# Decoding attention on one core: heads software-pipelined across the engines, K loaded one head ahead

## The chip, the core, the metric

One core of a Trainium2 chip. The metric is device time in microseconds (us) of one execution; lower is better. The kernel before takes 2669.79 us (median of 4 runs, 2669.45 to 2670.34). Repeats agree within 0.1%, so a few us can be seen, but only just.

## The reference

Two independent attention blocks (A and B) for one decoding step; their outputs are concatenated.

```python
# B=8 batches, 1 query, D=1024, H=32 heads, Sk=4096 keys, Dh=128, bfloat16
q = (x @ wq).reshape(B, 1, H, Dh).transpose(0, 2, 1, 3)
scores = einsum("bhqd,bhkd->bhqk", q, k_cache) * Dh ** -0.5
p = softmax(scores)
o = einsum("bhqk,bhkd->bhqd", p, v_cache)
out = o.transpose(0, 2, 1, 3).reshape(B, 1, H * Dh) @ wo
```

Every element of K and V is used once. Per head, K is 8 tiles of 1 MB (one a batch), and so is V. Over 64 heads that is 1.07 GB, read from memory once.

## The kernel before

One loop over heads n = 0..63. All loads are issued by SyncE (SP) on one queue. K tiles go into a ring of NK = 6 slots, V tiles into a ring of NV = 8. DVE transposes each K tile, PE multiplies it with q, then the softmax of the head goes DVE - PE - DVE - PE - ACT - DVE, then PE multiplies with V (pv), ACT evicts and scales, and PE projects with wo.

```python
# SP: all loads, in order
load_group(first[0])                       # wq of the first 4 heads: 8 DMAs of 128 KB
wait(sp, s_const, 1)                       # x_sb is zeroed by GpSimd first
... x ...
for n in range(NH):
    for b in range(Bsz):                   # K of head n
        t = n * Bsz + b
        wait(sp, s_tr, t - NK + 1)         # slot free: the tile NK back is transposed
        sp.dma_start(knat[:, t % NK, :], kc[b, h]...)
    ...                                    # every 4th head: wq; each head: wo, 256 KB
    for b in range(Bsz):                   # V of head n
        wait(sp, s_pv, t - NV + 1)         # slot free: the tile NV back has been multiplied
        sp.dma_start(vnat[:, t % NV, :], vc[b, h]...)

# PE, head n:    qk(n); max and bias matmuls; row sums; prep(n+1); pv(n); o^T; projection
# DVE, head n:   8 x transpose K; max; max of rows; transpose of e; reciprocal
```

Below, K(n,b) and V(n,b) are the tiles of head n and batch b, qk(n) and pv(n) are the two products of a head, pv(n,b) is the part of one batch.

## Time and profile before

| what | value | where it is read |
|---|---|---|
| time | 2669.79 us | runs |
| bytes read | 1107 MB, 415 GB/s over the span | page |
| DMA engines' busy share from 20 to 2650 us | 1.00 to 1.02 | windows |
| PE busy | 75% | page |
| DVE idle, waiting for a K tile | 1065 us | waits |
| full rate begins | about 10.6 us | windows of 1 us |

The page of the kernel before: busy time of the engines; then GB/s in 40 equal slices of the span; bytes; the chain of waits; and the two costliest groups (busy us, mean ns | idle us before them, and what ended the idle time).

```profile
PE 2009.5 (75%) x10880; PEld 729.3 (27%) x10880; DVE 1292.0 (48%) x781; ACT 263.3 (10%) x727; POOL 7.7 (0%) x17
...
GB/s 371 417 420 421 417 421 417 420 421 416 421 416 421 420 417 420 416 421 421 415 420 417 420 420 415 421 416 420 418 419 420 414 421 413 421 420 418 420 421 348
...
HBM read 1107.33 MB, written 0.03 MB: 415 GB/s over the span
...
DMA 81%; DVE 10%; SPq 6%; PE 2%; issue 1%; POOL 0%; ACT 0%; DVEq 0%; POOLq 0%
...
L249 DVE STREAM_TRANSPOSE kt<-knat 128x2048 f32<-128x2048 f32 x512 | 1170.9, 2303 | 1119.1 <-DMA knat<-in_B_k_cache_dram 536.7
L334 PE MATMUL ps<-kt,lpad 128*128 128x512 bf16 x4096 | 1021.6, 394 | 229.4 <-DVE kt L249 227.7
```

No compute engine is near full, and the chain of waits is DMA for 81%. DVE, which touches each K tile first, idled 1119 us, mostly for K tiles to land. The slices are at 413 to 421 GB/s except the first (371) and the last (348).

The windows view of the kernel before splits that up. Columns: stretch, its length, busy us (and count) of PE, PEld, DVE, ACT and POOL, granted PE clock, DMA busy share, GB/s.

```profile
0.00:10.00 10.00, 0.00 (x0) 0.00 (x0) 4.71 (x13) 0.00 (x0) 7.69 (x17) 1.00 0.35 108
10.00:40.00 30.00, 20.13 (x165) 7.52 (x165) 19.77 (x11) 4.78 (x12) 0.00 (x0) 1.00 1.00 413
40.00:60.00 20.00, 15.69 (x103) 5.66 (x99) 4.50 (x4) 2.66 (x7) 0.00 (x0) 0.86 1.01 421
60.00:70.00 10.00, 8.69 (x36) 3.17 (x34) 8.81 (x5) 0.00 (x0) 0.00 (x0) 0.93 1.01 422
70.00:100.00 30.00, 21.69 (x133) 7.89 (x132) 10.52 (x9) 3.90 (x11) 0.00 (x0) 0.92 1.01 420
100.00:2640.00 2540.00, 1925.60 (x10355) 698.62 (x10354) 1239.97 (x739) 248.05 (x688) 0.00 (x0) 0.93 1.01 419
```

Of these, only the first 10 us run far below the rest: 108 GB/s. The timeline of the start says why. Columns: start us, us, engine, line, operation, count, and in brackets the idle time before it and what ended it; SPq lines are DMA issues.

```profile
0.81 3.70 SPq L171 DMA_DIRECT2D wq_sb<-in_A_wq_dram  x8
...
8.16 0.20 POOL L225 TENSOR_SCALAR_AFFINE_SELECT selrow<-ones_bf 128x16 bf16<-128x16 bf16 x1
...
8.39 0.34 SPq L179 DMA_DIRECT2D x_sb<-in_A_x_dram  x1
...
9.10 9.85 SPq L189 DMA_DIRECT2D knat<-in_A_k_cache_dram  x8
...
18.82 3.65 PE L334 MATMUL ps<-kt,lpad 128*128 128x512 bf16 x16 [1.51 <-ACT lpad L424]
...
19.47 8.79 SPq L202 DMA_DIRECT2D vnat<-in_A_v_cache_dram  x8
```

The queue issues wq, then waits until GpSimd finishes its constants at 8.36 us (L225), issues x, and only at 9.10 us K. The first qk matmul runs at 18.82 us. V(0) is issued straight behind K(0), all eight tiles within 9 us.

The waits of the queue's own sequencer in the kernel before (us in total, times, longest):

```profile
SPq L189 <- DVE kt L249: 1189.8, 271, 15.9
```

The queue waits only for slots of K; it never once waits for a slot of V.

The Trainium skill ("DMA: Bandwidth & Descriptors", section Specifications) names a fabric ceiling of 435 GB/s and an HBM limit of about 358 GB/s per core, which it works out as half of what two cores share. This trace runs at 419 to 422 GB/s for 2.6 ms with only this core at work, so the second figure did not bind here; the measurement decides. That the limit is the 16 DMA engines and not the one queue in front of them is read from their busy share alone (1.00 to 1.02).

### The profile page before, as it was taken

What the parts mean: (1) busy time and instruction counts of PE and PEld (TensorE: products, weight loads), DVE (VectorE), ACT (ScalarE), POOL (GpSimd) and SP (SyncE); (2) the same over time, 40 slices, a digit from 0 to 9 for tenths busy, and PEclk for the clock granted to TensorE, in tenths of its full rate; (3) what the DMA queues carried; (4) which work ended last, traced back from release to release, by engine and by line L of the source; (5) the groups of instructions that cost most, each with busy time, mean ns of one, the idle gap of its engine ahead of it and who ended that gap; (6) DMA issues with size and microseconds to landing.
All of it is one profiled execution on the core that took longest, in us unless ns stands there. A gap on an engine that the chain in (4) does not pass through costs nothing.

```text
span 2667.7 us, 26152 instructions
## 1 busy us (share of the span) xinstructions
PE 2009.5 (75%) x10880; PEld 729.3 (27%) x10880; DVE 1292.0 (48%) x781; ACT 263.3 (10%) x727; POOL 7.7 (0%) x17
## 2 busy tenths in 40 slices
PE   6777777777777777777777777777777777777777
PEld 2222222222222222222222222222222222222222
DVE  5454544545535445354453544535535355363553
ACT  1001100011000110110101101011010100101001
POOL 1000000000000000000000000000000000000000
PEclk9998999999999989999999999999999899999989
DMA  9999999999999999999999999999999999999998
GB/s 371 417 420 421 417 421 417 420 421 416 421 416 421 420 417 420 416 421 421 415 420 417 420 420 415 421 416 420 418 419 420 414 421 413 421 420 418 420 421 348
DMA packets 175316, 1109.09 MB, mean 416 GB/s; under 512 B 19504, under 2 KB 35920, under 8 KB 44128
## 3 DMA queue, kind: packets, MB, share of 16 engines
q1 hardware_dynamic: 175136, 1107.41, 100.5%
q8 instruction: 86, 1.41, 0.2%
q14 instruction: 30, 0.25, 0.0%
q10 hardware_dynamic: 64, 0.03, 0.0%
HBM read 1107.33 MB, written 0.03 MB: 415 GB/s over the span
## 4 chain that ended last, share of the span: by engine, by line
DMA 81%; DVE 10%; SPq 6%; PE 2%; issue 1%; POOL 0%; ACT 0%; DVEq 0%; POOLq 0%
DMA knat<-in_B_k_cache_dram 39%; DMA knat<-in_A_k_cache_dram 37%; DVE kt L249 10%; SPq L189 3%; DMA vnat<-in_A_v_cache_dram 3%; DMA vnat<-in_B_v_cache_dram 2%; SPq L202 1%; SPq L171 1%; PE ps L334 1%; PE ps L289 0%; PE ps L372 0%; SPq L197 0%; POOL lpad L211 0%; ACT o_sb L452 0%; PE ps L394 0%
## 5 line engine op out<-in xcount | busy, mean ns | idle before, releaser
L249 DVE STREAM_TRANSPOSE kt<-knat 128x2048 f32<-128x2048 f32 x512 | 1170.9, 2303 | 1119.1 <-DMA knat<-in_B_k_cache_dram 536.7
L334 PE MATMUL ps<-kt,lpad 128*128 128x512 bf16 x4096 | 1021.6, 394 | 229.4 <-DVE kt L249 227.7
L372 PE MATMUL ps<-vnat,pq_sb 128*4 128x512 bf16 x4096 | 848.9, 433 | 119.8 <-DMA vnat<-in_A_v_cache_dram 61.3
L334 PEld LDWEIGHTS ps<-kt,lpad 128*128 128x128 bf16 x4096 | 367.3, 99 | 875.5 <-DVE kt L249 449.4
L372 PEld LDWEIGHTS ps<-vnat,pq_sb 128*4 128x4 bf16 x4096 | 292.2, 94 | 646.5 <-issue 152.1
L452 ACT ACTIVATE o_sb<-ps,rlo_sb 128x512 bf16<-128x512 f32 x128 | 80.9, 683 | 880.8 <-PE ps L372 880.8
L437 ACT ACTIVATE bias_sb<-ps 128x1 f32<-128x1 f32 x64 | 11.0, 171 | 1362.2 <-PE ps L347 1362.2
L253 DVE TENSOR_REDUCE m_sb<-ps 128x1 bf16<-128x512 f32 x64 | 44.4, 694 | 128.7 <-PE ps L334 128.7
L383 PE MATMUL ps<-selrow,o_sb 128*128 128x4 bf16 x512 | 22.6, 166 | 86.9 <-ACT o_sb L452 86.9
L261 DVE STREAM_TRANSPOSE pq_sb<-e_sb 128x512 bf16<-128x512 bf16 x64 | 45.5, 711 | 83.7 <-ACT e_sb L441 83.7
L424 ACT ACTIVATE lpad<-ps 32x32 bf16<-32x32 f32 x256 | 77.9, 304 | 70.3 <-PE ps L306 65.6
L354 PE MATMUL ps<-l1m_sb,maskcg 128*32 128x2 f32 x512 | 16.5, 188 | 90.5 <-ACT l1m_sb L445 90.5
L342 PE MATMUL ps<-ident,m_sb 128*1 128x128 bf16 x64 | 13.9, 217 | 50.3 <-DVE m_sb L253 50.3
L383 PEld LDWEIGHTS ps<-selrow,o_sb 128*128 128x128 bf16 x512 | 17.0, 96 | 119.0 <-ACT o_sb L452 119.0
L441 ACT ACTIVATE e_sb<-ps,bias_sb 128x512 bf16<-128x512 f32 x64 | 44.0, 687 | 2.1
L289 PE MATMUL ps<-wq_sb,xT_sb 128*8 128x512 bf16 x128 | 39.6, 466 | 0.0
L394 PE MATMUL ps<-wo_sb,oT_sb 128*8 128x512 bf16 x128 | 24.9, 386 | 17.1 <-ACT oT_sb L456 17.1
L354 PEld LDWEIGHTS ps<-l1m_sb,maskcg 128*32 128x32 f32 x512 | 11.0, 118 | 95.9 <-ACT l1m_sb L445 95.9
L306 PE MATMUL ps<-ident,q_pad 128*32 128x8 bf16 x1024 | 17.4, 170 | 24.9 <-DVE rlo_sb L264 24.2
L347 PE MATMUL ps<-scalecol,negm 128*32 128x1 bf16 x256 | 12.0, 177 | 23.9 <-DVE negm L257 23.9
L257 DVE TENSOR_REDUCE negm<-ps 1x16 bf16<-1x128 f32 x64 | 18.0, 281 | 19.8 <-PE ps L342 19.8
L342 PEld LDWEIGHTS ps<-ident,m_sb 128*1 128x1 bf16 x64 | 5.1, 79 | 82.1 <-DVE m_sb L253 82.1
(37 smaller groups left out, 119.6 us busy)
## 6 DMA issues: line engine op xcount, KB each, us to landing
knat<-in_A_k_cache_dram SPq DMA_DIRECT2D x256, 1024.0 KB, 26.4
vnat<-in_A_v_cache_dram SPq DMA_DIRECT2D x256, 1024.0 KB, 20.8
knat<-in_B_k_cache_dram SPq DMA_DIRECT2D x256, 1024.0 KB, 26.5
vnat<-in_B_v_cache_dram SPq DMA_DIRECT2D x256, 1024.0 KB, 20.9
wq_sb<-in_A_wq_dram SPq DMA_DIRECT2D x64, 128.0 KB, 10.1
wo_sb<-in_A_wo_dram SPq DMA_DIRECT2D x32, 256.0 KB, 12.8
wq_sb<-in_B_wq_dram SPq DMA_DIRECT2D x64, 128.0 KB, 9.0
wo_sb<-in_B_wo_dram SPq DMA_DIRECT2D x32, 256.0 KB, 12.9
```

The source lines that it names most:

```text
L189: sp.dma_start(knat[:, slot, :], kc[b, h].rearrange("(p j) d -> p (j d)", p=128),).then_inc(s_kld[slot], 16)
L249: dve.transpose(kt[:, ts, :].bitcast(F32), knat[:, ks, :].bitcast(F32)).then_inc(s_tr, 1)
L253: dve.tensor_reduce(m1_sb[:], S_ps[par], axis=AX.X, op=ALU.max).then_inc(s_m1, 1)
L261: dve.transpose(pq_sb[:], e_sb[:]).then_inc(s_pq, 1)
L289: last = pe.matmul(q_ps[G % 2], lhsT=xT_sb[:, blk, ch, :], rhs=wq_sb[:, G % 2, ch, :], start=(ch == 0), stop=(ch == NCH - 1))
L334: last = pe.matmul(S_ps[par], lhsT=lpad[:, b, c, 2 - 2 * g:2 - 2 * g + 128], rhs=ktv[:, 16 * g:16 * g + 16, bq, :, e_], start=(b == 0 and ...
L354: last = pe.matmul(Lq_ps[32 * cg:32 * cg + 32, :], lhsT=maskcg[:, 32 * cg:32 * cg + 32], rhs=l1m_sb[:, :], start=True, stop=True, tile_pos ...
L372: last = pe.matmul(O_ps[slot][32 * cg:32 * cg + 4, :], lhsT=pq_sb[:, base:base + 97:32], rhs=vnat[:, vs, j0 * 128:(j0 + 4) * 128], start=( ...
L383: last = pe.matmul(oT_ps[:, slot * 4:slot * 4 + 4], lhsT=o_sb[:, slot, m * 128:(m + 1) * 128], rhs=selrow4[:, m, :], start=(m == 0), stop= ...
L424: act.activation(dst, src, ACT.Identity).then_inc(s_lp, 1)
L441: act.activation(e_sb[:], S_ps[par], ACT.Exp, bias=bias_sb[:], scale=SCALE, accum_out=l1_sb[:]).then_inc(s_exp, 1)
L452: act.activation(o_sb[:, slot, :], O_ps[slot], ACT.Identity, scale=rlo_sb[:, slot:slot + 1]).then_inc(s_oev, 1)
```

## The change

The intent: PE should not stand idle during a head's softmax. So qk(n+1) and the maximum of head n+1 are put ahead of pv(n), and K is loaded one head ahead. With it come smaller edits: x takes 8 partitions in place of a zeroed 128, so that nothing waits for the constants at the start; wq comes as one DMA of 1 MB in place of eight; q is copied into a replicated layout with 16 small ACT operations a group in place of one; NK goes from 6 to 7 and NV from 8 to 6.

```diff
-NK = 6
+NK = 7
-NV = 8
+NV = 6
-LEAD = 2
+LEAD = 3
 # SP
-            load_group(first[0])
-            wait(sp, s_const, 1)
             for blk in range(NBLK): ... x ...
+            load_group(first[0])            # one DMA, 1 MB
+            load_k(0)
             for n in range(NH):
-                ... K of head n ...
+                if n + 1 < NH:
+                    load_k(n + 1)
                 ... wq, wo, V of head n ...
 # GpSimd
-            pool.memset(x_sb[:], 0.0)       # 128 x 2048
-            pool.memset(q_pad[:], 0.0)      # 128 x 1024
+            pool.memset(q_rep[:], 0.0)      # 128 x 4096
             pool.memset(lpad[:], 0.0)       # 128 x 4224
 # PE
-            for n: qk(n); max; bias; row sums; prep(n+1); pv(n); o^T; projection
+            prep(0); qk(0); smax_a(0); smax_b(0); prep(1)
+            for n in range(NH):
+                if n + 1 < NH:
+                    qk(n + 1)
+                    smax_a(n + 1)           # max and bias
+                for b in range(Bsz):
+                    pv(n, b)
+                smax_b(n + 1); prep(n + 2); otr(n); outproj(n)
 # ACT: q copy
-                act.activation(q_pad[0:8, G % 2, :], q_ps[G % 2], ACT.Identity)
+                for hl in range(HPG):
+                    for a_ in range(4):
+                        act.activation(q_rep[0:8, ...], src[:, hl], ACT.Identity)
... (PSUM layout, semaphores and the order of ACT and DVE to match)
```

## The prediction

> **What bounds the kernel now.** DMA. The windows view gives 417 to 423 GB/s and a DMA share of 1.01 to 1.02 in every stretch from 20 to 2650 us. The chain of waits is 81% DMA. Compute follows: DVE waits 1065 us for K tiles, PE is busy 75%. The Trainium skill, "DMA: Bandwidth & Descriptors", section Specifications, names a fabric ceiling of 435 GB/s and an HBM limit per core of about 358; this trace's 421 GB/s is 97% of the first and above the second, so the rate has little left. The change moves the same 1107 MB.
>
> What is not at full rate in the trace:
> - The start. By one-microsecond windows the first wq group moves from 2 to 6 us, the queue is empty from 7 to 9 us (x waits for the constants, K for x), and full rate begins at about 10.6 us.
> - The tail. The last bytes land at 2659.5 us, and 8 us of PV, eviction, projection and store follow.
> - 16 wq groups: around each about 0.85 us is lost (1 KB packets take 49 ns, 8 KB ones 314).
>
> **What the change does.**
> 1. Heads overlap: qk(n+1) and its max run before pv(n). This takes the softmax chain (36.9 to 40.7 us in head 0) off PE's path. PE is idle waiting for DMA anyway: worth 0.
> 2. K one head ahead is a new order, consumed in the same order. NK+NV falls from 14 to 13 tiles. In steady state V(n,6) needs pv(n,0), about 8 to 9 us after the last K tile landed, with six V tiles (15 us) queued: no starvation. Worth 0.
> 3. x, wq and K no longer wait for constants: K streams from about 5.8 instead of 10.6 us. Gain about 4.8 us.
> 4. But compute starts no earlier. Zeroing q_rep (4096 columns, about 3.5 us, from lpad's 3.6 for 4224) puts the constants at about 9.5 us; the q copy becomes 16 small ACT operations of about 0.28 us (4.5 us, was 0.59). First qk at about 19.9 us (was 18.8). Then, at DVE's 2.27 us per K tile, K(1,7) is issued only after K(1,0) is transposed, about 43 us, and V(0,6) only after pv(0,0), now behind all of qk(1), about 65 us, though the queue ran dry at about 61. So new stalls of 2 and 3 us in the first 70 us hand the gain back. Net at the start: 0, give or take 2 us.
> 5. wq as one DMA: fewer completions (1792 of 10 ns over 16 engines, 1 us), perhaps fewer issue gaps; against that, successive 1 KB packets now lie 1 MB apart. Sign open.
> 6. Tail: unchanged, 8 us.
>
> **Prediction: 2669 us, range 2661 to 2677. Faster by over 2%: 1%; within 2%: 98%; slower: 1%.**
>
> **What would show it.** DMA share 1.0 and 420 GB/s in all windows from 80 us on; full rate from about 6 us; dips in GB/s near 43 and 62 to 68 us; first qk at 19 to 21 us; PE busy little changed; V issues waiting on PV in the queue's waits; the span from the last V landing to the end still about 8 us.
>
> **What would make it wrong.** wq reads slower at their new pitch (2x would cost 3 us per group, 45 us); a steady V starvation with six slots, which would show as dips each 41 us; or a start without stalls, which would give 2664.

## The result, and the profile after

2669.09 us (median of 9 runs, 2668.73 to 2669.51) against 2669.72 us for the kernel before beside it (13 runs, 2669.01 to 2670.34). The ratio is 0.9998, 95% interval 0.9988 to 1.0007: the same. (A ratio here is the mean time of one kernel's runs over that of the other's of the same rounds, so not quite the ratio of the medians quoted.) The prediction was 2669.

The page of the changed kernel, the same parts. Its chain of waits broke off after a handful of links (all shares 0%), so it can't be used here.

```profile
PE 2060.1 (77%) x9728; PEld 745.3 (28%) x9728; DVE 1269.7 (48%) x775; ACT 295.9 (11%) x967; POOL 8.5 (0%) x16
...
GB/s 371 419 420 418 420 421 418 421 417 421 421 417 420 415 419 421 417 419 417 420 421 417 417 417 420 421 418 418 417 419 421 417 418 417 419 421 414 421 421 347
...
L261 DVE STREAM_TRANSPOSE kt<-knat 128x2048 f32<-128x2048 f32 x512 | 1156.6, 2293 | 1115.7 <-DMA knat<-in_B_k_cache_dram 507.0
L334 PE MATMUL ps<-kt,lpad 128*128 128x512 bf16 x4096 | 1039.8, 400 | 154.7 <-DVE kt L261 153.1
```

PE now idles only 155 us before the qk matmuls in place of 229. But by the same pages it idles 202 us before the pv matmuls in place of 120, and 99 us before the projection in place of 17: much of the idle time has moved, and not gone. The span doesn't notice: the slices have nearly the same GB/s from end to end.

The windows view of the changed kernel:

```profile
0.00:10.00 10.00, 0.88 (x65) 0.73 (x66) 2.00 (x8) 1.73 (x3) 8.51 (x16) 1.00 0.75 272
10.00:40.00 30.00, 21.01 (x83) 7.28 (x82) 19.04 (x11) 5.08 (x24) 0.00 (x0) 1.00 1.02 422
40.00:60.00 20.00, 15.73 (x67) 5.84 (x67) 17.92 (x10) 1.22 (x4) 0.00 (x0) 0.91 1.00 411
60.00:70.00 10.00, 8.31 (x62) 3.28 (x61) 1.68 (x3) 1.25 (x4) 0.00 (x0) 1.00 0.67 252
70.00:100.00 30.00, 23.41 (x104) 8.48 (x103) 19.60 (x12) 3.90 (x11) 0.00 (x0) 0.88 1.02 415
100.00:2640.00 2540.00, 1973.29 (x9269) 713.56 (x9267) 1209.29 (x733) 278.64 (x913) 0.00 (x0) 0.96 1.01 419
```

Read these six lines against those of before. In the first 10 us the changed kernel moves 272 GB/s in place of 108, and 422 in place of 413 in the next 30. Then 411 in place of 421, and 252 in place of 422 from 60 to 70 us. Over the first 100 us the mean is 386 GB/s, against 387 before. The gain and the loss cancel. From 100 us on both are at 419.

A rate rounded to 1 GB/s can hide 3 us over those 2540 us, as much as is at stake here. So I added up the windows view in steps of 5 us. The table gives how many us of bytes (at 419 GB/s) each kernel has moved more than the kernel before by a given time, and in the last column how much sooner its profiled execution ended (before: 2669.45). The sums are good to about 0.3 us; the runs e1 to e12 are explained below.

| kernel | by 40 us | by 70 us | by 150 us | by 2640 us | end |
|---|---|---|---|---|---|
| changed kernel | 4.5 | 0.1 | 0.2 | 0.6 | 0.7 |
| e2: changed, NV 8 | 4.5 | 3.2 | 3.4 | 4.1 | 4.3 |
| e3: changed, NK 8, NV 8 | 4.5 | 4.5 | 4.5 | 5.2 | 5.6 |
| e4: changed, K issued late | -0.2 | -1.4 | -1.8 | -2.3 | -1.2 |
| e7: changed, constants sooner | 4.5 | 2.3 | 2.6 | 3.0 | 3.5 |
| e1: before, early issue | 2.8 | 2.7 | 2.8 | 1.6 | 2.2 |
| e6: e1, one wq DMA | 4.5 | 4.5 | 4.6 | 4.2 | 4.1 |
| e12: e6, NK 8, NV 8 | 4.4 | 4.4 | 4.5 | 4.5 | 4.7 |

In sizes, by windows of 10 us: at 20 us the changed kernel is 1.9 MB ahead (2.72 + 4.22 MB against 1.08 + 3.98), which at 421 GB/s is 4.5 us. By windows of 1 us, the bytes missing from 43 to 47 us are worth 0.6 us, and those missing from 61 to 68 us 4.1 us (from 62 to 65 us the rates are 49, 16 and 0 GB/s). That gives 4.5 - 4.7 us, about nothing.

The timeline of the start of the changed kernel shows who empties the queue:

```profile
1.59 0.41 SPq L171 DMA_DIRECT2D wq_sb<-in_A_wq_dram  x1
2.03 40.69 SPq L182 DMA_DIRECT2D knat<-in_A_k_cache_dram  x16
...
9.56 0.22 DVE L247 TENSOR_SCALAR maskslot<-iota,pf 128x2 f32<-128x2 f32 x1
...
13.58 2.62 ACT L446 ACTIVATE q_rep<-ps 8x128 bf16<-8x128 f32 x16 [9.21 <-PE ps L301]
...
17.99 5.21 PE L334 MATMUL ps<-kt,lpad 128*128 128x512 bf16 x16 [1.47 <-ACT lpad L458]
...
40.10 2.27 DVE L261 STREAM_TRANSPOSE kt<-knat 128x2048 f32<-128x2048 f32 x1
...
43.24 22.37 SPq L209 DMA_DIRECT2D vnat<-in_A_v_cache_dram  x8
...
61.05 0.69 DVE L267 TENSOR_REDUCE m_sb<-ps 128x1 bf16<-128x512 f32 x1 [2.01 <-PE ps L334]
...
62.50 6.25 PE L372 MATMUL ps<-vnat,pq_sb 128*4 128x512 bf16 x48
```

K's issue begins at 2.03 us in place of 9.10. But the constants (last one at 9.56 us) hold up q: its matmuls begin at 9.89 us, the sixteen copies take 2.62 us (L446), and the first qk is at 17.99 us, barely earlier than 18.82. From there on K is consumed at DVE's pace. The sixteen K issues last until 42.7 us, as the last one, K(1,7), needs the slot of K(1,0), whose transposition runs from 40.10 to 42.37. Then V: its eight issues take from 43.24 to 65.6 us. Six are free at once; the seventh needs pv(0,0), and pv(0) starts at 62.50, after all of qk(1) and its maximum (61.05). The six tiles had run out at 62.

The waits of the queue's sequencer in the changed kernel:

```profile
SPq L209 <- PE ps L372: 947.6, 134, 18.8
SPq L182 <- DVE kt L261: 756.1, 71, 14.0
```

V slots are now waited for, 134 times. That looks alarming and costs next to nothing after the start (from 150 to 2640 us the changed kernel does not fall behind the kernel before, and behind e2, with eight slots, by some 0.5 us at most): while the sequencer waits, up to six issued V tiles are still being moved. A wait of the issuer counts only when what it has issued runs out, and that shows in GB/s, not in this view.

### The profile page after: what moved, and what is told of

Same layout as the page of the kernel before. It is cut to its first block, busy times and chain, and to the rows that moved or that the text cites. A ratio compares the mean times of both kernels' runs of the same rounds, so it can differ in the third digit from the quotient of the medians.

```text
span 2667.0 us, 24031 instructions
## 1 busy us (share of the span) xinstructions
PE 2060.1 (77%) x9728; PEld 745.3 (28%) x9728; DVE 1269.7 (48%) x775; ACT 295.9 (11%) x967; POOL 8.5 (0%) x16
## 2 busy tenths in 40 slices
DMA packets 173518, 1108.97 MB, mean 416 GB/s; under 512 B 17712, under 2 KB 34128, under 8 KB 42336
## 5 line engine op out<-in xcount | busy, mean ns | idle before, releaser
L261 DVE STREAM_TRANSPOSE kt<-knat 128x2048 f32<-128x2048 f32 x512 | 1156.6, 2293 | 1115.7 <-DMA knat<-in_B_k_cache_dram 507.0
L334 PE MATMUL ps<-kt,lpad 128*128 128x512 bf16 x4096 | 1039.8, 400 | 154.7 <-DVE kt L261 153.1
L372 PE MATMUL ps<-vnat,pq_sb 128*4 128x512 bf16 x4096 | 878.2, 380 | 201.7 <-DMA vnat<-in_B_v_cache_dram 100.7
L334 PEld LDWEIGHTS ps<-kt,lpad 128*128 128x128 bf16 x4096 | 373.2, 100 | 814.4 <-DVE kt L261 350.5
L372 PEld LDWEIGHTS ps<-vnat,pq_sb 128*4 128x4 bf16 x4096 | 299.3, 87 | 750.9 <-DMA vnat<-in_B_v_cache_dram 186.5
L301 PE MATMUL ps<-wq_sb,xT_sb 128*8 128x512 bf16 x128 | 47.3, 537 | 5.8 <-DVE maskslot L247 5.8
L446 ACT ACTIVATE q_rep<-ps 8x128 bf16<-8x128 f32 x256 | 41.9, 250 | 58.7 <-PE ps L301 58.7
L399 PEld LDWEIGHTS ps<-wo_sb,oT_sb 128*8 128x8 bf16 x128 | 5.5, 82 | 104.6 <-ACT oT_sb L485 104.6
L357 PEld LDWEIGHTS ps<-l1m_sb,maskcg 128*128 128x128 f32 x128 | 19.0, 188 | 28.9 <-issue 27.4
```

What stands on the lines that cost most here:

```text
L261: dve.transpose(kt[:, ts, :].bitcast(F32), knat[:, ks, :].bitcast(F32)).then_inc(s_tr, 1)
L301: last = pe.matmul(q_ps, lhsT=xT_sb[:, blk, ch, :], rhs=wq_sb[:, G % 2, ch, :], start=(ch == 0), stop=(ch == NCH - 1))
L334: last = pe.matmul(S_ps[par], lhsT=lpad[:, b, c, 2 - 2 * g:2 - 2 * g + 128], rhs=ktv[:, 16 * g:16 * g + 16, bq, :, e_], start=(b == 0 and ...
L372: last = pe.matmul(O_ps[slot][32 * cg:32 * cg + 4, :], lhsT=pq_sb[:, m % 2, base:base + 97:32], rhs=vnat[:, vs, j0 * 128:(j0 + 4) * 128], ...
L399: last = pe.matmul(OUT_ps[c], lhsT=oT_sb[:, :], rhs=wo_sb[:, ws, c * OW:(c + 1) * OW], start=(h == 0), stop=(h == H - 1), tile_position=(0 ...
L446: ins = act.activation(dst, src[:, hl], ACT.Identity)
```

## The experiments

My theory: the kernel is bound by the bytes of one DMA queue; only the empty queue at the start, and the tail, can be won; the change wins at the start and loses the same in its first two heads, because compute does not start earlier, and its order of loads with six V slots then runs dry. Rivals: the early start is worth nothing; the overlap gains and something else (six slots in every head, or the new wq reads) loses.

| kernel | us (median) | ratio to before | 95% interval |
|---|---|---|---|
| changed kernel | 2669.09 | 0.9998 | 0.9988 to 1.0007 |
| e1: before, early issue | 2667.25 | 0.9991 | 0.9978 to 1.0003 |
| e6: e1, one wq DMA | 2665.24 | 0.9985 | 0.9973 to 0.9998 |
| e12: e6, NK 8, NV 8 | 2664.95 | 0.9984 | 0.9970 to 0.9998 |
| e2: changed, NV 8 | 2664.31 | 0.9979 | 0.9965 to 0.9993 |
| e3: changed, NK 8, NV 8 | 2663.65 | 0.9977 | 0.9964 to 0.9989 |
| e4: changed, K issued late | 2669.78 | 1.0000 | 0.9988 to 1.0013 |
| e7: changed, constants sooner | 2666.05 | 0.9986 | 0.9972 to 1.0000 |
| e5: e3, eight wq DMAs | 2666.35 | 0.9986 | 0.9972 to 0.9999 |
| e8: before, NV 4 | 2888.85 | 1.0831 | 1.0812 to 1.0850 |
| e9: changed, NV 4 | 2723.66 | 1.0204 | 1.0190 to 1.0218 |
| e10: e3, shorter tail | 2661.74 | 0.9970 | 0.9958 to 0.9983 |
| e11: e3, 2 MB DMAs | 2664.27 | 0.9982 | 0.9970 to 0.9995 |

All were correct. Differences of 1 to 8 us are all within 0.3%. I lean on a difference of a few us only where the trace shows it at the place where it should be.

### e1: the early issue alone, in the kernel before

```diff
-            pool.memset(x_sb[:], 0.0)       # x_sb now has 8 partitions
-            load_group(first[0])
-            wait(sp, s_const, 1)
             for blk in range(NBLK): ... x ...
+            load_group(first[0])
```

> Kernel before with one part of the change alone: x, then wq, then K are issued at once (x in 8 partitions, no wait for the constants). No overlap of heads, old order and old rings (NK 6, NV 8). My theory (the DMA queue is the bound; early issue is worth 4 to 5 us; the changed kernel loses it again in stalls that its order makes in the first 70 us): V(0) stands right behind K(0) with 8 free slots, so no stall; about 2665 us, 4 to 5 below before, full rate from about 6.5 us on and no dip. Rival (the early start is worth nothing, for instance because the tail or the slowest DMA engine sets the end): 2669 to 2670. Rival (the overlap of heads gains and something else of the change loses): early issue alone gives less than 2 us.

2667.25 us (2666.22 to 2668.49): less than expected. In its trace no stall follows, as predicted, but the rates from 2 to 12 us are only 161, 263, 223, 377 and 369 GB/s: the eight wq issues take 3.67 us of the sequencer, so K comes at 5.30 us. Over the first 100 us the mean is 399 GB/s against 387, worth 2.9 us. Its interval includes 1, so by time alone this run settles nothing.

### e2 and e3: more slots in the changed kernel

```diff
-NV = 6
+NV = 8      # e2
-NK = 7
+NK = 8      # e3, with NV = 8
```

> Changed kernel with NV 8 in place of 6, nothing else. My theory: V(0,6) and V(0,7) no longer wait for pv(0,0), so the empty queue from 62 to 66 us goes away and only the dip at 43 to 46 us stays; about 2665 us, 4 us below the changed kernel, all of it before 80 us. Rival (six V slots starve the queue a little in every head): the gain is spread over all heads and larger than 4 us. Rival (the slots don't matter, the loss is in the wq reads): 2669.

> Changed kernel with NV 8 and NK 8. My theory: K(1,7) needs no transposed K(1,0) any more, only K(0,7), at about 35 us, so the dip at 43 to 46 us (about 1 us) goes as well; about 2664 us, no dip before 80 us. Rival (slots don't matter): 2669.

2664.31 us and 2663.65 us. Two lines of the windows view of e2:

```profile
40.00:60.00 20.00, 15.88 (x62) 5.87 (x62) 18.24 (x10) 1.73 (x7) 0.00 (x0) 0.83 0.96 394
60.00:70.00 10.00, 8.57 (x69) 3.64 (x70) 1.92 (x4) 1.25 (x4) 0.00 (x0) 1.00 1.01 419
```

The same two lines of e3:

```profile
40.00:60.00 20.00, 16.02 (x64) 6.05 (x65) 18.04 (x10) 1.22 (x4) 0.00 (x0) 0.85 1.01 421
60.00:70.00 10.00, 8.84 (x73) 3.67 (x72) 1.69 (x3) 1.25 (x4) 0.00 (x0) 1.00 1.02 421
```

With eight V slots the stretch from 60 to 70 us has 419 GB/s in place of 252, and the dip before it stays, even deeper (394 against 411; why is open). With eight K slots as well the dip goes too (421). By 70 us e2 is 3.1 us and e3 4.4 us ahead of the changed kernel, and their profiled executions end 3.6 and 4.9 us sooner, so most of the gain lies where the theory put it. From 150 us on six slots cost at most 0.5 us against eight, and the rival with a loss in every head falls. The medians (4.8 us, then 0.7 more) are near the 4 and 1 us expected.

### e4: the early issue taken away again, in the changed kernel

```diff
                 load_group(G)
+            sp.wait_ge(s_const, 1)
             load_k(0)
```

> Changed kernel, but K(0) is issued only when the constants are ready (about 9.3 us), x and wq early as before. My theory: in the changed kernel the time of the first 66 us is set by compute (first qk at 18 us, then pv(0,0) at 64 us releases V(0,6)), so K 4 us later costs nothing: same as the changed kernel within 1 us, 2669, with an empty queue from 6 to 10 us and a shorter one near 62 us. Rival (early issue is worth its 4 to 5 us in the changed kernel and is lost elsewhere): 2673 to 2674.

2669.78 us, the same as the changed kernel within 0.7 us. Two lines of its windows view:

```profile
0.00:10.00 10.00, 0.88 (x65) 0.73 (x66) 1.78 (x7) 1.73 (x3) 8.52 (x16) 1.00 0.35 108
...
60.00:70.00 10.00, 8.57 (x62) 3.60 (x61) 2.07 (x4) 1.25 (x4) 0.00 (x0) 1.00 0.94 374
```

The first 10 us are as slow as in the kernel before (108 GB/s in place of the changed kernel's 272, 3.9 us of bytes at 421 GB/s), and from 60 to 70 us the rate is 374 in place of 252 (2.9 us); the dip near 43 us is gone as well. Most of what was taken from the start came back by 70 us, not all: e4 is 4.8 us behind the changed kernel by 40 us, 1.4 by 70, and 2.0 by 150, and the two profiled executions (2670.66, the slowest of e4, and 2668.73, the fastest of the changed kernel) end 1.9 us apart. So in the changed kernel as it stands the early issue is worth 0.7 us by the medians and at most some 2 by the traces, and not 4.5: for the most part compute sets the time of its first two heads.

### e7: compute starts sooner, no DMA touched

```diff
-            pool.memset(lpad[:], 0.0)       # GpSimd
+            dve.memset(lpad[:], 0.0)        # DVE, beside GpSimd
```

> Changed kernel (NK 7, NV 6), lpad zeroed by DVE beside GpSimd's other constants in place of after them. My theory: in the changed kernel the first 66 us are set by when compute starts. The constants are ready at about 7.2 in place of 9.8 us, the first qk moves from 18.0 to about 15.4, V(0,6) is released as much sooner, and the whole kernel ends 2 to 2.7 us sooner: about 2666.5. No DMA is touched. Rival (the empty queue at 62 us has nothing to do with the start of compute): 2669.

2666.05 us, 3.0 us less than the changed kernel. The timeline of its start (q matmul, first qk, first pv), and one line of its windows view:

```profile
7.10 3.57 PE L301 MATMUL ps<-wq_sb,xT_sb 128*8 128x512 bf16 x8 [3.05 <-DMA wq_sb<-in_A_wq_dram]
...
15.21 5.76 PE L334 MATMUL ps<-kt,lpad 128*128 128x512 bf16 x16 [1.47 <-ACT lpad L458]
...
60.20 6.25 PE L372 MATMUL ps<-vnat,pq_sb 128*4 128x512 bf16 x48
```

```profile
60.00:70.00 10.00, 8.82 (x63) 3.48 (x64) 0.75 (x2) 1.25 (x4) 0.00 (x0) 1.00 0.83 329
```

The first two come 2.8 us earlier (7.10 in place of 9.89, 15.21 in place of 17.99), pv(0) 2.3 us earlier (60.20 in place of 62.50), and the empty stretch shrinks with it: 329 GB/s from 60 to 70 us in place of 252. By 70 us e7 is 2.2 us ahead of the changed kernel; the median ends 3.0 us earlier. What ends the wait of the q matmul is now the wq DMA.

### e6 and e12: the early issue in the kernel before, mended

```diff
 # e1, and
-                for ch in range(NCH):
-                    sp.dma_start(wq_sb[:, G % 2, ch, :], wq[ch * 128:(ch + 1) * 128, ...])
+                sp.dma_start(wq_sb[:, G % 2, :, :], wq.rearrange("(ch p) n -> p ch n", p=128)[...])
 # e12 only
-NK = 6
+NK = 8
```

> As e1_before_early, and wq as one DMA a group. In e1 the eight wq issues took 3.7 us of the issuing queue, so K followed at 5.3 us and 100 us on, only 2.9 us of bytes had been gained. My theory (early issue is the whole gain, the overlap of heads is worth nothing while DMA is the bound): one issue lets K follow at 2 us; 2664 to 2665, within 1.5 us of e3 (overlap, no stall). Rival (the overlap of heads is worth some us of its own): stays 2 us or more above e3's 2663.6.

> e6 (kernel before, early issue, one wq DMA a group, no overlap of heads) ended 1.6 us above e3 (overlap of heads), 2665.2 against 2663.6. They differ in two things: overlap, and 14 against 16 slots. This is e6 with NK 8 and NV 8, so the slots are equal. If the 1.6 us come from the slots[...]: 2663.2 to 2664.2. If they come from the overlap of heads, or the order of K and V: 2665 again.

2665.24 us and 2664.95 us. That is 4.1 and 4.6 us less than the kernel before of the same rounds (2669.37 and 2669.51), without any overlap of heads, from the start alone (275 GB/s in the first 10 us, and no dip after it). e3, with the overlap, ends 1.3 us before e12 with the same slots (1.9 us by the ratios, 0.9977 against 0.9984). The expectation of e6 left this between my theory (within 1.5 us) and the rival (2 us or more), and e12 took the slots out as a cause. What the 1.3 to 1.9 us are stays open. The two runs were made on different chips; in their traces e3 is 0.1 us ahead by 70 us and 0.7 by 2640 us. So the overlap of heads is worth at most some 2 us of 2669 here, and not shown to be worth that.

### e5: is the single wq DMA slower to read?

```diff
 # e3, and
-                sp.dma_start(wq_sb[:, G % 2, :, :], ...)   # PE's wait counts eight DMAs again
+                for ch in range(NCH):
+                    sp.dma_start(wq_sb[:, G % 2, ch, :], ...)
```

> e3 (changed kernel, NK 8, NV 8: no stall at the start) with wq back to eight DMAs a group. My theory: costs 2 us at the start (eight issues take 3.7 us in place of 0.4, K follows later), and within 1 us nothing over the other 15 groups: 2665 to 2667. Rival (the single DMA's 1 KB packets, 1 MB apart, are slower to read, which the eight would mend): 2663 or less. Rival (the single DMA saves a lot in every group): 2672 or more.

2666.35 us (in two bunches, 2664.6 and 2666.7), 2.7 us more than e3, as the start demands: 206 GB/s in its first 10 us against 274 in e3, worth 1.6 us of the 2.7; the rest was not traced. From 100 us on both have 419 GB/s. A packet of 1 KB takes 50.0 ns on average in e3 and 48.9 in e5; over 16416 packets and 16 engines that is 1.1 us. The Trainium skill ("DMA: Bandwidth & Descriptors", section Latency and other measured facts) reports copies between HBM tensors that get slower as the row pitch per partition grows in powers of two (207 GB/s at 512 KiB, 164 at 2 MiB). There the pitch is from partition to partition; here that is 8 KB in both forms, and only the packets of one partition lie 1 MB apart, so it is not the page's case. They took only 2% longer, so the 45 us that the prediction named as a danger did not come.

### e8 and e9: where the overlap does pay

```diff
-NV = 8      # kernel before (e8);  -NV = 6  changed kernel (e9)
+NV = 4
```

> Kernel before with NV 4: four V slots. Where the bound is the queue, the order of the work on PE matters only through when it frees slots. In the kernel before pv(n,0) ends 10 to 11 us after the last K tile landed (the softmax chain and a cold PE in between), and four V tiles with wo last 10.6 us, less about 1.5 us from issue to data. My theory: the queue runs dry in every head by 1 to 4 us: 2730 to 2900, best guess 2800. If the slots don't matter: 2669.

> Changed kernel with NV 4. pv(n,0) ends 7.9 us after the last K tile landed, as the softmax of head n was done one head ago, and PE is warm; with 1.5 us from issue to data that is inside the 10.6 us that four tiles last. My theory: only the start loses more, and the 16 heads with a q group may lose 1 to 2 us: 2672 to 2705. So the overlap is worth about 100 us where slots are scarce, and nothing where they are not. Rival (the overlap does not shorten the time to free a slot): as e8, 2730 or more.

2888.85 us (inside the expected range, 89 above the best guess) and 2723.66 us: with four V slots the changed kernel is 165 us faster. Three lines of the timeline of e8, one head:

```profile
1066.30 2.31 DVE L249 STREAM_TRANSPOSE kt<-knat 128x2048 f32<-128x2048 f32 x1 [0.20 <-DMA knat<-in_A_k_cache_dram]
...
1074.38 5.86 PE L372 MATMUL ps<-vnat,pq_sb 128*4 128x512 bf16 x32
...
1077.69 3.05 SPq L202 DMA_DIRECT2D vnat<-in_A_v_cache_dram  x4
```

The last K tile begins to be transposed at 1066.30 us. pv of the head begins at 1074.38, after the softmax, and the next V issue is at 1077.69: 11.4 us later, and by the 1 us windows the queue is empty from 1076 to 1078. The 3.3 us from the start of pv to the issue are eight matmuls on a cold PE (414 ns each; the windows view has a granted clock of 0.56 there). The Trainium skill ("TensorE: Matmul & The Clock Gate", section Wait — 56ns, not 53.3ns?) gives 426.7 ns start to start for 512 columns when cold and 215.7 when warm; other groups of eight in this trace take 1.91 us.

The same place in e9, the group of the last qk, and pv:

```profile
1029.07 1.92 PE L334 MATMUL ps<-kt,lpad 128*128 128x512 bf16 x8 [0.44 <-DVE kt L261]
...
1032.47 4.25 PE L372 MATMUL ps<-vnat,pq_sb 128*4 128x512 bf16 x24
...
1034.39 5.15 SPq L209 DMA_DIRECT2D vnat<-in_A_v_cache_dram  x4
```

Here pv follows the last qk (1029.07) by 3.4 us, on a PE that was just busy (granted clock 1.00 from 1026 to 1036 us), and the V issue comes 1.9 us after the start of pv. In e8 the last qk was at 1068.67, pv 5.7 us behind it, and the V issue another 3.3. My numbers for e9 (2672 to 2705) were too low: I had expected only the start and the heads with wq to lose; its trace has, from 300 to 1400 us, a dip of 0.4 to 1.5 us in most heads and of 1.0 to 3.8 us in those with wq. The direction and the order of size hold. The overlap is not isolated here: the two kernels also differ in NK (6 and 7) and in the smaller edits. But in the dry stretch of e8 the issuer waits for a V slot, and the six K issues behind it go out without a wait, so one more K slot would not have filled it.

### e10 and e11: what else is to be had

e10 works on the tail of e3:

```diff
+                    if t == NH * Bsz - 1:    # the very last V tile in four DMAs, one semaphore each
+                        for i in range(4):
+                            sp.dma_start(vnat[:, slot, 1024 * i:1024 * (i + 1)], ...).then_inc(s_vlast[i], 16)
-                act.wait_ge(s_pv, (m + 1) * Bsz)
                 for slot in range(2):
+                    act.wait_ge(s_pv, m * Bsz + 4 * slot + 4)   # evict each half when its 4 batches are done
... (PE waits for the four parts one by one)
```

> e3 (NK 8, NV 8) with the tail worked on: the very last V tile comes as four DMAs with a semaphore each, and the first half of o is evicted when its four batches are done. In e3 eight matmuls (1.9 us) and two evictions (1.26 us) follow the last landing; here two matmuls (0.5 us) and one eviction (0.6 us). My theory: 1.5 to 2 us less than e3, about 2661.8. Rival (the end is set by the slowest DMA engine's store path): no change, 2663.6.

2661.74 us, 1.9 us less than e3. The end of e3, the pv that the last landing releases, and the eviction:

```profile
2654.50 1.39 PEld L372 LDWEIGHTS ps<-vnat,pq_sb 128*4 128x4 bf16 x8 [1.06 <-DMA vnat<-in_B_v_cache_dram]
...
2656.43 1.27 ACT L479 ACTIVATE o_sb<-ps,rlo_sb 128x512 bf16<-128x512 f32 x2 [18.55 <-PE ps L372]
```

The end of e10:

```profile
2654.24 0.10 PEld L379 LDWEIGHTS ps<-vnat,pq_sb 128*4 128x4 bf16 x2 [0.54 <-DMA vnat<-in_B_v_cache_dram]
...
2654.88 0.69 ACT L486 ACTIVATE o_sb<-ps,rlo_sb 128x512 bf16<-128x512 f32 x1 [7.93 <-PE ps L379]
```

In e3 the eviction is 1.27 us long and comes after a last group of eight matmuls; in e10 two matmuls and one half of the eviction (0.69 us) remain. From the last landing's release to the end it is 7.6 us in e3 (2654.50 to 2662.1) and 5.8 in e10 (2654.24 to 2660.0), so 1.8 of the 1.9 us are in the tail, as expected.

e11 loads K and V in pairs:

```diff
-                    sp.dma_start(knat[:, slot, :], kc[b, h]...)
+                    sp.dma_start(knat[:, slot:slot + 2, :], kc[b:b + 2, h].rearrange("b (p j) d -> p b (j d)", p=128))
... (V the same; one semaphore a pair)
```

> e3 with K and V loaded in pairs, 2 MB a DMA, so half of the 4-byte completion writes (9.6 ns each; 16384 of them over 16 engines are about 10 us of engine time). If a completion takes the engine's time, 4 to 5 us less in the steady part, less about 2 us in a coarser tail: about 2661. If it overlaps with the data: no gain and 1 to 2 us lost at both ends: 2665 to 2667.

2664.27 us (in two bunches, 2664.3 and 2666.1), nothing gained, though just under the 2665 to 2667 expected for that case: 9520 packets under 512 B (nearly all of them completions) in place of 17712, and still 419 GB/s from 100 us on. So the completions did not cost what their busy time suggests.

**e10 beats both kernels:** 2661.74 us, 0.9970 of the kernel before (0.9958 to 0.9983). It is 0.3%. The ends are not used up by it: in e10 too the rate falls before the last landing, from 361 GB/s at 2647 us to 39 at 2653, worth 3.8 us of bytes. No run tried to mend that, and its cause was not looked for.

## Why the prediction was right

- *DMA bounds the kernel, and the rate has little left.* Right. 419 GB/s from 100 us on in the kernel before, the changed kernel, and all variants with enough slots.
- *Overlap of heads: worth 0.* Right within 2 us. e12 (no overlap) and e3 (overlap) are 1.3 us apart. e8 and e9 show that with the overlap V slots come free sooner, which pays where they are scarce.
- *Six V slots in steady state: worth 0.* Right within 0.5 us: e2 is 3.1 us ahead of the changed kernel by 70 us and 3.5 by 2640 us.
- *Early issue gains 4.8 us.* 4.5 us by the bytes at 20 us.
- *Compute starts no earlier.* Right, with two wrong sizes inside. The sixteen q copies took 2.62 us, not 4.5, so the first qk was at 18.0 us, not 19.9. Against that, the first sixteen qk matmuls took 5.21 us, where the kernel before had shown 3.65. The two errors nearly cancelled; V(0,6) was issued at 64.4 us, where I had said about 65.
- *Stalls of 2 and 3 us.* 0.6 and 4.1 us: the sum was right (4.7 against 5), its parts were not, so the match of the sum is luck too. K(1,0) was transposed by 42.4 us, close to the 43 that I had said, so a late or early start of compute does not explain the short first stall; I did not take it apart.
- *wq as one DMA: sign open.* It is worth 2 to 3 us when nothing hides the start (e1 against e6, e3 against e5), and about 1 us of slower packets against it.
- *Tail 8 us, unchanged.* From the start of the last pv group to the end 7.6 us before and 7.8 after. I left out that the rate falls over the 7 us before the last landing, in both kernels alike.

That the time came out at 2669.1 for 2669 is luck to the last us; that it would not move was not, and e2, e4 and e7 show the cancellation with one edit each (e4 all but 0.7 to 2 us of it).

## What to carry to other kernels

When one queue of loads is full from end to end, reordering the compute can win nothing but the stretches in which that queue is empty: look for those first, in GB/s by small windows, and cost the rest at zero. A prefetch one step deeper changes which consumer frees which slot; work through the first two iterations by hand, since there compute lags most and an early start of the loads may be handed back as an empty queue a little later. Software pipelining and buffer slots are two currencies for the same slack: with four V slots the changed kernel was 165 us faster, with enough of them the overlap was worth at most 2.

## What the Trainium skill lacked or had wrong

- "DMA: Bandwidth & Descriptors", section Specifications, gives the HBM limit of about 358 GB/s per core without saying that it holds only with both cores of a pair streaming; that stands further down the page. Of loads from HBM the section Bandwidth also says that "the HBM side (~358) binds". With one core alone it did not: 419 to 422 GB/s for 2.6 ms, 97% of the page's fabric ceiling of 435.
- The same page has 408.7 GB/s for a stream of 1 MiB loads with 4 KiB rows on one core. It lacks longer rows and larger loads in a stream: 1 MB loads with 8 KB rows held 419 GB/s here, and 2 MB loads no more (e11).
- No page has in us what an issue costs the issuing queue (the same page has 512 cycles a DMA for "previous generations"): eight of 128 KB took 3.67 us at the start, one of 1 MB with the same 1 KB rows 0.41 us, and K followed at 5.30 against 2.03 us.
- No page has how a wait of the issuing sequencer is to be read in a trace: 948 us of waits for V slots in the changed kernel cost no more than about 0.5 us beyond the first 70 us.
